# One fused block (modulated local attention and MLP) on one core: the hand-off order of 713 tasks and their buffer slots is replaced by another

## The chip, the core and the metric

The kernel runs on one core of a Trainium2 chip. The core's engines run side by side and meet only through semaphores: TensorE (PE) multiplies matrices and writes only to PSUM, VectorE (DVE), ScalarE (ACT) and GpSimd (POOL) do the rest of the arithmetic, and SyncE (SP) issues DMAs. Each engine takes its own instructions strictly in the order in which the program gives them. The metric is device time in microseconds; lower is better. Verdicts here call two kernels the same within 2%.

## What is computed

The input x has 2048 rows of 448 bfloat16 values. A vector c gives six modulation vectors. A layernorm, scaled and shifted by them, feeds an attention with 16 heads of 28 values in which row s looks at rows s, s−2, ..., s−14; its result is projected by wo, gated and added to x. A second modulated layernorm, and a third without modulation, feed an MLP of 1792 hidden values with a tanh GELU, gated and added again.

```python
mod = (_silu(c) @ w_mod).reshape(c.shape[0], 6, 1, -1)
sa, ca, ga, sb, cb, gb = (mod[:, i] for i in range(6))
h = _layernorm(x) * (1 + ca) + sa
qkv = (h @ wqkv)                       # 16 heads of 28; W, dil = 8, 2
idx = pos[:, None] - (jnp.arange(8) * 2)[None, :]
attn = softmax(where(idx >= 0, q . k[idx] * 28 ** -0.5, -1e9))
x = x + ga * ((attn . v[idx]) @ wo)
h = _layernorm(x) * (1 + cb) + sb
x = x + gb * (gelu(_layernorm(h) @ w1 + b1) @ w2 + b2)
```

## The kernel before

**Tiles.** The rows are split into even and odd ones, so that the dilated window becomes a plain window of 8 in each half. A tile p (0 to 7) is 128 even and 128 odd rows. `hT`, `qT` and `kT` hold the normalised rows, the queries and the keys with the features on the partitions.

**Stages.** For each tile DVE computes the statistics (L456 and L458) and normalises (L478); the reciprocal root of the variance is one power on POOL (L469) or two steps on ACT (L466, L467). A short copy, the "tail" (L488 to L492, on DVE, POOL or ACT), doubles the last 64 features. Tiles 0 and 1 are then transposed by PE (L535), tiles 2 to 7 by a DMA of SP (`zT`, L527), and scaled and shifted into `hT` (L502 on DVE, L504 on ACT; four per group of tiles, one for each quarter of the features). Queries and keys are projected by PE in two parts, full quarters (L548) and the remainder of 64 features (L554). For tiles 0 and 1 the result is copied straight into `qT` and `kT` (L609 on ACT, L610 on DVE). For tiles 2 to 7 it is copied into one of five staging buffers `zy` (L628 on ACT, L629 on DVE) and transposed into `qT` or `kT` by a DMA (L631).

The attention runs in nine batches of 114 positions of each half: values (L706 for batches 0 to 4; from a copied window `hw`, L689, and with L548 and L554 for 5 to 8), copied to `vb` (L721 on ACT, L724 on DVE); two sets of logits (`lt`, L738); exponentials (L745, ACT); mask (L751, DVE); denominators (`pd`, L760) and weighted values (`po`, L771); logarithm and exponential of the denominator (L780, L782, ACT); product (L788, DVE). The output projection (`pw`, L803) of a tile, the sum with x (L810) and the two layernorms (L819 applies the modulation) follow, and a transpose by DMA (`yT`, L834).

The MLP takes two tiles at a time, t = 0 to 3: 14 hidden tiles in pairs (g, g+7), two pairs to a group, named here by g: 0/1, 2/3, 4/5, 6. Each pair has full matmuls (L548) and remainder matmuls (L554) into one PSUM slot, and two GELUs on ACT (L864) that read that slot; the bias column for them is copied out of PSUM by DVE (L671). Then follow the second matmul (L883), the biased residual on POOL (L841, behind a gate L868) and the last add (L889) and the store (L893). Three phases interleave these: attention batches 0 to 4 and MLP 0, batches 5 and 6 and MLP 1, batches 7 and 8 and MLPs 2 and 3. ACT loads another table between exponentials and GELUs (L925, L932).

**What sets the order.** The code records 713 tasks (`Plan.add`), each with its engine, its inputs and outputs, and for some of them other engines that could do it (`alt`). Nothing is scheduled while the program is built. `emit` goes through a fixed list of task numbers, `ORDER`, and calls each; `:A`, `:D` and `:P` after a number put it on ACT, DVE or POOL, and `:R` reverses the two parts of a values task. So the list fixes each engine's order. `SLOTS` gives each buffer its slot among a few of its kind (`ROOM`): four PSUM slots P0 to P3 of two banks each (projections, logits, values, GELU inputs, all of them), five `zy`, two `et`, two `den`, two `hw` and so on. The first writer of a slot waits for all readers of the buffer that was in it before.

Of the kernel before, what the change touches and what calls it, by code (L numbers as in the profile page):

```python
# [14 lines left out]
S, D, H, DH, F = 2048, 448, 16, 28, 1792  # L15
# [25 lines left out]
ENGINE = {"A": "ACT", "D": "DVE", "P": "POOL", "R": "PE2"}  # L41
RATE = 310e3
SLOTS = [
# [6 lines left out]
]  # L50
ORDER = """
3 14 17 0 1 15 5 9 10 18 11 16 13 19 20 2 6 24 21 73 55+12@55 26 12 71 25 56 72 74 57 75 22 58 77 23 59 60 27 62 61 76
32 4 67 66 68+11@68 78 63 28 108 64 30 110 69 79 84:A 89:P 31 65 70 109 111 80 88:P 83 34 81 112:P 87:A 29 101+9@101
85 90:A 93:P 36 114 94+3@94 82 95 113 102 92:A 91 115:D 86 103 116 96 120:A 144 97 99 104 106 117:A 135 98 118:A 142
105 119:A 145 143 133 100 146 121 136 134 126 148 137 107 147 7 127 149:D 122 138 124 150 129 139 190 123 191 140 198
141 128 125 200 199 269 130 271 236 40 270 207 33 209 38 241 201 35 237 208 210 185 211 154 39 153 242 202 152 212
151:A 8 203 187 213 238 204 159 239 214:D 205 215 186 240 155 278 206 188 279 280 156 160 307:R 161 281 243 37 282 272
192 273:A 162 157 189 171 308:D 194 172 283 193 244 218 173 195 163 219 158 275 284 196 216 285 167 217 286 447:P 246
197 164 168 165 228 174 169:D 274 309 312 276:D 277 220 313 310 314 166 221 229 225 230 311 224 222:D 247 170 315 245
176 317 316 175 226 248 233 232 318 227 290 249 289:A 319 43 287:A 223 288 320 234 250 558:P 46 45 559 321 47 231 253  # L60
345 342 346 251 560 303 482:P 44 252 324 343 322 291 561 254 323 325 347 326 344 292 304 255 293 327 348 328 373:R 256
305 294 329 257 350 258 375 52 378 376 330 340:R 53 333 379 235 377 374 296 334 331 300 41 295 351 332 259 49 335 380
299 341 336 337 297 260 382 262 301 381 349 263 261 264 338:A 383 483 352 339 384 265 484 266 449 353 267 485 385 268
# [3 lines left out]
402 452 404 443 487 453 370 490 454 444 436 455 371:D 372 456 434 491 405 488 457 493 445 459 458 492 460 435 494 461  # L67
# [3 lines left out]
513 547 515:D 599 516 564 602 568 481 569 570 604 603 571 546 605 572 548 606 573 628 607 608 574 549 635 575 550 609  # L71
612 636 577 630 637 578 610 629 640 576 579 638 581 639 611 613 580 582 641 631 583 633 586 651 614 632 587 584 585
616 588 642 615 648 617 654 646 647 618 634 652 645 656 621 649 619 644 622 620 623 643 658 650 625 624 589 626 664
590 655 627 591:A 653 657 439 592 659 556 665 662 663 674 666 660 661 669 667 675 668 678 676 679 677 686 672 673 671
687 681 670 680 690 691 694 697 693 682 688 692 685 695 683 689 701 684 698 696 709 699 710 702 711 712 705 700 703
706 704 707 708
"""


# [883 lines left out]
```

## Time and profile before

| | us |
|---|---|
| median of 3 runs | 171.04 |
| the runs | 169.43, 171.04, 171.4 |
| span of the profiled execution, first to last instruction | 166.6 |
| what lies around the span, if that execution took the median | 4.4 |

The page gives the span of one execution but not its device time, so the last row is a difference between two executions. DVE and ACT are busy 116.1 and 102.4 us, POOL 46.7 us. DMA engines are nearly full for the first 62 us (all inputs and weights are loaded there, among the transposes) and near idle from then on. A row of the timeline has the start, the duration, the engine, the line, what is written from what, the count, and in brackets the idle time of that engine just before and what ended it. A row such as "1.78 ... x2" covers both instructions; the second starts about half of that after the first, so that rows of several give the rate at which an engine gets through them. PE's matmuls overlap, so their rate is read from where the next row starts.

### The profile page before, as it was taken

The page shows a single profiled execution, that of the slowest core. Times are in us where ns is not written, and L with a number is a line of the kernel's source. Part 1 is how long each engine was busy: PE and PEld are TensorE (multiplying, and loading weights), DVE is VectorE, ACT ScalarE, POOL GpSimd, SP SyncE. Part 2 cuts the span into 40 slices and gives each one's busy share as a digit, 9 for nine tenths or more (in the row PEclk, how much of TensorE's full clock was granted, in tenths as well). Part 3 has the DMA queues.
Part 4 walks back from the last instruction along what each step waited for, and adds up shares of the span by engine and source line. Part 5 has one row for each costly group of instructions (what it writes and reads, how often), then busy time and mean ns, then how long its engine had stood idle before and what let it go on. Part 6 is the DMA issues. An engine that isn't in the chain of part 4 may idle for free.

```text
span 166.6 us, 4971 instructions
## 1 busy us (share of the span) xinstructions
PE 160.9 (97%) x2126; PEld 83.7 (50%) x2126; DVE 116.1 (70%) x271; ACT 102.4 (61%) x142; POOL 46.7 (28%) x73
## 2 busy tenths in 40 slices
PE   6999899999999999999999999999999999999992
PEld 4678544444545543445555344556434455344572
DVE  6889899958899989996938886574788930500032
ACT  3378898798489953859674468947536820097300
POOL 3136332300261201289100114700002870007200
PEclk9999999999999999999999999999999999999999
DMA  5999989799999999900091000009010026110003
GB/s 152 323 335 311 182 269 172 147 160 190 222 185 306 147 161 245 151 0 6 2 139 46 4 0 0 4 0 126 8 55 0 0 55 185 64 46 0 0 1 110
DMA packets 35573, 18.78 MB, mean 113 GB/s; under 512 B 28507, under 2 KB 34592, under 8 KB 35552
## 3 DMA queue, kind: packets, MB, share of 16 engines
q1 hardware_dynamic: 35548, 18.47, 51.0%
q8 instruction: 16, 0.26, 0.7%
q14 instruction: 5, 0.04, 0.1%
q10 hardware_dynamic: 4, 0.00, 0.0%
HBM read 9.81 MB, written 1.84 MB: 70 GB/s over the span
## 4 chain that ended last, share of the span: by engine, by line
PE 88%; DMA 4%; ACT 2%; SPq 2%; POOL 1%; DVE 1%; issue 1%
PE p L883 26%; PE p L548 22%; PE pq L548 8%; PE pw L803 8%; PE pv L706 5%; PE p L554 4%; PE lt L738 4%; PE po L771 3%; PE pv L548 3%; DMA wqk_st<-in_A_wqkv_dram 3%; PE pq L554 2%; DMA kT<-zy 2%; PE pd L760 1%; SPq L349 1%; PE pb L641 1%
## 5 line engine op out<-in xcount | busy, mean ns | idle before, releaser
L864 ACT ACTIVATE hm<-p,b_col 128x512 bf16<-128x512 f32 x56 | 33.9, 692 | 29.9 <-PE p L554 27.3
L883 PE MATMUL p<-w_s,hm 128*128 128x448 bf16 (+1 forms) x238 | 44.1, 342 | 0.0
L548 PE MATMUL p<-yT,w_s 128*128 128x512 bf16 x168 | 38.1, 380 | 0.0
L469 POOL TENSOR_TENSOR rs_all<-mvs,neg_half 128x2 f32<-128x2 f32 x22 | 16.7, 764 | 58.0 <-DVE mvs L458 57.9
L883 PEld LDWEIGHTS <-hm 128*128 128x128 bf16 x238 | 22.6, 98 | 19.3 <-issue 0.8
L889 DVE TENSOR_TENSOR x_all<-p,x1p 128x896 bf16<-128x896 f32 (+2 forms) x10 | 8.9, 902 | 25.9 <-PE p L883 25.9
L548 PEld LDWEIGHTS <-w_s 128*128 128x128 bf16 x168 | 15.8, 98 | 20.9 <-issue 2.9
L456 DVE BATCH_NORM_STATS2 stt<-x_all 128x6 f32<-128x448 bf16 x32 | 18.6, 608 | 0.8 <-DMA x_all<-in_A_x_dram 0.6
L745 ACT ACTIVATE et<-lt 128x928 bf16<-128x928 f32 x18 | 16.0, 947 | 4.2 <-PE lt L738 3.9
L841 POOL TENSOR_TENSOR x1p<-x_all,gbb_bc 128x448 f32<-128x448 bf16 x16 | 17.8, 1137 | 0.0
L548 PE MATMUL pq<-wqk_st,hT 128*128 128x448 bf16 x72 | 15.0, 354 | 0.0
L788 DVE TENSOR_TENSOR qT<-po,den 128x912 bf16<-128x912 f32 x9 | 10.0, 1106 | 6.6 <-ACT den L782 6.4
L751 DVE TENSOR_TENSOR et<-et,mask 128x928 bf16<-128x928 bf16 x18 | 11.8, 683 | 3.1 <-ACT et L745 3.0
L803 PE MATMUL pw<-wo_s,qT 128*128 128x448 bf16 x64 | 13.3, 353 | 0.0
L780 ACT ACTIVATE den<-pd 128x928 f32<-128x928 f32 x9 | 8.5, 943 | 5.9 <-PE pd L760 5.7
L819 DVE TENSOR_TENSOR h<-h,mod_bc 128x896 bf16<-128x896 bf16 x16 | 11.1, 710 | 0.3
L628 ACT CAST zy<-pq 128x896 bf16<-128x896 f32 x10 | 8.9, 912 | 1.7 <-PE pq L554 0.9
L548 PEld LDWEIGHTS <-hT 128*128 128x128 bf16 x72 | 6.4, 98 | 6.9 <-issue 1.6
L782 ACT ACTIVATE den<-den,den_bias 128x928 f32<-128x928 f32 x9 | 9.6, 1072 | 0.2
L478 DVE TENSOR_SCALAR zy<-h,mvs,rs_all 128x448 bf16<-128x448 bf16 x16 | 6.6, 457 | 4.4 <-POOL rs_all L469 4.4
L810 DVE TENSOR_TENSOR x_all<-pw,x_all 128x896 bf16<-128x896 f32 x8 | 8.7, 1086 | 1.3 <-PE pw L803 1.3
L456 DVE BATCH_NORM_STATS2 stt<-h 128x6 f32<-128x448 bf16 x16 | 9.4, 612 | 0.2
(115 smaller groups left out, 182.0 us busy)
## 6 DMA issues: line engine op xcount, KB each, us to landing
w_s<-in_B_w_dram SPq DMA_DIRECT2D x7, 224.0 KB, 3.8
out_dram<-x_all SPq DMA_DIRECT2D x7, 224.0 KB, 2.1
x_all<-in_A_x_dram SPq DMA_DIRECT2D x3, 448.0 KB, 5.3
wmod<-in_w_mod_dram SPq DMA_DIRECT2D x3, 448.0 KB, 7.2
w_s<-in_B_w_dram SPq DMA_DIRECT2D x3, 448.0 KB
wqk_st<-in_A_wqkv_dram SPq DMA_DIRECT2D x3, 225.0 KB, 3.9
wm_st<-in_w_mod_dram SPq DMA_DIRECT2D x1, 672.0 KB, 4.6
x_all<-in_A_x_dram SPq DMA_DIRECT2D x2, 224.0 KB, 2.6
```

Of the source, the lines that this page charges most:

```text
L456: add("DVE", 0.53, lambda: nc.vector.bn_stats(out=stt[:, w, b, 0:6], in_=src()), reads=reads, bufs=bufs, after=early if w == b == 0 else ( ...
L469: ways = {"POOL": (0.55 + 0.17 * n, lambda: nc.gpsimd.tensor_tensor(out=r, in0=v, in1=neg_half[:, 0:n], op=ALU.pow))}
L548: nc.tensor.matmul(out(), lhsT=lhs(kt, slice(0, 128)), rhs=rhs(kt, slice(0, 128)), start=first and kt == 0, stop=not first and kt == KT - 2)
L554: nc.tensor.matmul(out(), lhsT=lhs(KT - 1, rows), rhs=rhs(KT - 1, rows), start=first, stop=not first, tile_position=(rows.start, 0))
L745: exps.append(add("ACT", 0.83, lambda half=half, lt=lt: nc.scalar.activation(out=et.t[:, 2 * half:2 * half + 2].rearrange("p r m c -> p r ...
L751: nc.vector.tensor_tensor(out=ev, in0=ev, in1=mask[:], op=ALU.mult)
L788: nc.vector.tensor_tensor(out=qT[:, :, LEAD + q00:LEAD + q00 + 2 * WQ], in0=po.t[:, :, 0:NS * 4 * WQ].rearrange("p j (m c) -> p m j c", c=WQ),
L803: nc.tensor.matmul(pw.t[:, s, 0:D], lhsT=qT[:, KT * s + ft, LEAD + 128 * p:LEAD + 128 * p + 128], rhs=wo_s[:, ft, :], start=(ft == 0), sto ...
L819: add("DVE", 0.55, lambda vec=vec, op=op: nc.vector.tensor_tensor(out=h2.t[:], in0=h2.t[:], in1=vec.unsqueeze(1).to_broadcast([128, NS, D] ...
L841: add("POOL", 1.0, lambda n=n: nc.gpsimd.tensor_tensor(out=x1p.t[:, n, :], in0=xn(p, n), in1=gbb2_bc[:], op=ALU.add), reads=[f"x{p}", "gbb ...
L864: gelus.append(add("ACT", 0.585, lambda f=f, a=a, p1=p1s[g]: nc.scalar.activation(out=hm.t[:, f].rearrange("p n c -> p (n c)"), in_=p1.t[: ...
L883: nc.tensor.matmul(p2.t[:, n, 0:c1 - c0], lhsT=hm.t[:, f, n, q * 128:(q + 1) * 128], rhs=w2_s[:, f, c0:c1], start=(f == parts[0][0]), stop ...
```

## The change

`SLOTS` and `ORDER` are replaced; all code, all tasks and the loads' sizes stay. [...] The first hundred or so tasks stand as before.

```diff
 SLOTS = [
-    0, 0, 1, 1, 0, 0, 0, 0, 1, 2, 3, 0, 1, 0, 2, 3, 0, 3, 2, 1, 0, 1, 0, 2, 3, 1, 2, 1, 2, 3, 4, 1, 1, 0, 0, 3, 0,
+    0, 0, 1, 1, 0, 0, 0, 0, 1, 2, 3, 0, 1, 0, 2, 3, 0, 2, 3, 3, 0, 1, 0, 3, 3, 1, 2, 1, 1, 0, 2, 2, 1, 2, 0, 1,
...
 ORDER = """
 3 14 17 0 1 15 5 9 10 18 11 16 13 19 20 2 6 24 21 73 55+12@55 26 12 71 25 56 72 74 57 75 22 58 77 23 59 60 27 62 61 76
 32 4 67 66 68+11@68 78 63 28 108 64 30 110 69 79 84:A 89:P 31 65 70 109 111 80 88:P 83 34 81 112:P 87:A 29 101+9@101
-85 90:A 93:P 36 114 94+3@94 82 95 113 102 92:A 91 115:D 86 103 116 96 120:A 144 97 99 104 106 117:A 135 98 118:A 142
+85 90:A 93:P 36 114 94+3@94 82 95 113 102 92:A 91 115:D 86 103 116 96 120:A 144 97 99 104 106 117:A 135 7 105 119:A
...
```

What that does to the engines shows in the order of the instructions. Three places matter below.

First, DVE at the start of the attention, from the statistics of tiles 2 and 3 to the scaling of these tiles into `hT` (L502). Before:

```order
L456 BN_STATS stt<-x_all 128x6
L458 BN_AGGR mvs<-stt 128x2 x2
L478 TENSOR_SCALAR zy_96<-x_all,mvs,rs_all 128x448 x2
L491 COPY zy_96<-zy_96 128x2x64
L478 TENSOR_SCALAR zy_97<-x_all,mvs,rs_all 128x448 x2
L456 BN_STATS stt<-x_all 128x6 x2
L458 BN_AGGR mvs<-stt 128x2
L456 BN_STATS stt<-x_all 128x6 x2
L458 BN_AGGR mvs<-stt 128x2
L456 BN_STATS stt<-x_all 128x6 x2
L458 BN_AGGR mvs<-stt 128x2 x3
L502 TENSOR_SCALAR hT<-zT,mod_col 128x2x256 x3
```

Now, in the same stretch:

```order
L456 BN_STATS stt<-x_all 128x6 x2
L458 BN_AGGR mvs<-stt 128x2 x2
L456 BN_STATS stt<-x_all 128x6
L478 TENSOR_SCALAR zy_96<-x_all,mvs,rs_all 128x448 x2
L456 BN_STATS stt<-x_all 128x6
L478 TENSOR_SCALAR zy_97<-x_all,mvs,rs_all 128x448 x2
L456 BN_STATS stt<-x_all 128x6 x3
L458 BN_AGGR mvs<-stt 128x2 x2
L456 BN_STATS stt<-x_all 128x6 x2
L478 TENSOR_SCALAR zy_96<-x_all,mvs,rs_all 128x448
L458 BN_AGGR mvs<-stt 128x2
L610 CAST kT<-pq 128x8x128
```

More statistics stand ahead of and between the normalisations of tiles 2 and 3, and behind all of it, ahead of L502, stands the copy of tile 1's keys, which ACT made before (L609). One of the three scalings of L502 goes to ACT.

Second, ACT in the middle of the attention, around the scaling of tiles 6 and 7 into `hT` (L504). Before:

```order
L780 ACTIVATE den<-pd 128x928
L628 CAST zy_97<-pq 128x32x28
L782 ACTIVATE den<-den,den_bias 128x928
L504 ACTIVATE hT<-zT,mod_col 128x2x256 x2
L628 CAST zy_100<-pq 128x32x28
L745 ACTIVATE et<-lt 128x928 x2
```

Now:

```order
L628 CAST zy_96<-pq 128x32x28
L628 CAST zy_100<-pq 128x32x28
L780 ACTIVATE den<-pd 128x928
L782 ACTIVATE den<-den,den_bias 128x928
L504 ACTIVATE hT<-zT,mod_col 128x2x256 x3
L628 CAST zy_98<-pq 128x32x28
L504 ACTIVATE hT<-zT,mod_col 128x2x256
L628 CAST zy_96<-pq 128x32x28
L745 ACTIVATE et<-lt 128x928 x2
```

All four scalings of these tiles are on ACT now. The copy of tile 4's queries (to `zy_98`) moved from ahead of the reciprocal to behind three of them, and the copy of tile 5's queries (to `zy_96`) behind the fourth.

Third, PE in the first group of the MLP. The number behind `p1` is the buffer. Before, the full matmuls of group 4/5 (`p1_1649` takes the slot of a pair of group 2/3, whose GELUs it waits for) come behind the twelve full matmuls of group 0/1 (`p1_1616` is its second pair), whose remainders were done ahead of them:

```order
L548 MATMUL p1_1616<-yT_1534,w1_s_76 128x512
L548 LDWEIGHTS w1_s_76
L548 MATMUL p1_1616<-yT_1534,w1_s_76 128x512
L548 LDWEIGHTS w1_s_76
L548 MATMUL p1_1649<-yT_1534,w1_s_76 128x512 [waits Activation_49]
```

Now the remainders of group 0/1 (`p1_1621` is its second pair, in P3) come last and those of group 4/5 right behind (`p1_1650` in P1, `p1_1653` in P3):

```order
L554 MATMUL p1_1621<-yT_1470,w1_r_77 128x512
L554 LDWEIGHTS w1_r_77
L554 MATMUL p1_1650<-yT_1470,w1_r_77 128x512
L554 LDWEIGHTS w1_r_77
L554 MATMUL p1_1650<-yT_1470,w1_r_77 128x512
L554 LDWEIGHTS w1_r_77
L554 MATMUL p1_1653<-yT_1470,w1_r_77 128x512 [waits Activation_49]
```

The wait for ACT, for the two GELUs that read the slot P3, now stands three matmuls behind the last matmul that these GELUs need. In the third MLP ACT's GELUs also stand in another order: one of the first pair of group 0/1 stands between the two of its second pair.

More of the change, by code (lines that the diff above doesn't have):

```diff
@@ L53 @@
 32 4 67 66 68+11@68 78 63 28 108 64 30 110 69 79 84:A 89:P 31 65 70 109 111 80 88:P 83 34 81 112:P 87:A 29 101+9@101
-85 90:A 93:P 36 114 94+3@94 82 95 113 102 92:A 91 115:D 86 103 116 96 120:A 144 97 99 104 106 117:A 135 98 118:A 142
-105 119:A 145 143 133 100 146 121 136 134 126 148 137 107 147 7 127 149:D 122 138 124 150 129 139 190 123 191 140 198
-141 128 125 200 199 269 130 271 236 40 270 207 33 209 38 241 201 35 237 208 210 185 211 154 39 153 242 202 152 212
-151:A 8 203 187 213 238 204 159 239 214:D 205 215 186 240 155 278 206 188 279 280 156 160 307:R 161 281 243 37 282 272
@@ L58 @@
[L58 to L62, printed above, removed]
@@ L63 @@
-299 341 336 337 297 260 382 262 301 381 349 263 261 264 338:A 383 483 352 339 384 265 484 266 449 353 267 485 385 268
[3 rows of a table removed]
-402 452 404 443 487 453 370 490 454 444 436 455 371:D 372 456 434 491 405 488 457 493 445 459 458 492 460 435 494 461
[3 rows of a table removed]
-513 547 515:D 599 516 564 602 568 481 569 570 604 603 571 546 605 572 548 606 573 628 607 608 574 549 635 575 550 609
-612 636 577 630 637 578 610 629 640 576 579 638 581 639 611 613 580 582 641 631 583 633 586 651 614 632 587 584 585
-616 588 642 615 648 617 654 646 647 618 634 652 645 656 621 649 619 644 622 620 623 643 658 650 625 624 589 626 664
@@ L74 @@
-590 655 627 591:A 653 657 439 592 659 556 665 662 663 674 666 660 661 669 667 675 668 678 676 679 677 686 672 673 671
-687 681 670 680 690 691 694 697 693 682 688 692 685 695 683 689 701 684 698 696 709 699 710 702 711 712 705 700 703
-706 704 707 708
+85 90:A 93:P 36 114 94+3@94 82 95 113 102 92:A 91 115:D 86 103 116 96 120:A 144 97 99 104 106 117:A 135 7 105 119:A
+142 98 118:A 136 145 133 107 127 122 269 121 134 100 143 280 123 146 137:A 187 147 190 148 200 126 149:A 191 150 139
+128 138 271 188 140 124 129 8 278 236:R 141 125 198 201 199 207 202:A 33 185 237 209 35 203 37 270 130:D 38 151:A 154
@@ new lines @@
+241 153 152:A 238 208 272 210 242 204 159 211 205:A 273 213 186 206 155 279 212 281 189 214:A 239 192 215 160 156
+161:D 171 157 193 243 172 158 307 240 282:A 195 284 162 244 196 308:D 194 167 39 246 219 217 173 283 218:A 163 197 40
+285:A 216:A 286 247 275 168 221 164 169:D 229 165 174 228 274 276:D 277 309 312 310 220 166 313 311 232 222 314 170
+176 230 245 315 223 233 248 225 317 224 175 318 41 316 288:A 249 319 290:A 289:A 226 320 250 287:A 227 234 558:P 251
+345 321 342 231 482:P 303 343 322 346 46 253 292 560 44 252 304 254 291 347 305 47 255 323 43 324 559 42 257 293 325
@@ new lines @@
+256 235 326 258 375 259 378 260 45 340:R 379 262 376 327 344 373 561 328 329 341 330 296 263 348 333 374 295 377 350
+331 299 332 334 297 380 335 447 349 351 337 381 261 300 336 484 383 264 352 483 338 384 339 266 265 382 267:D 406
+593:P 353 385 268 485:D 386 51 52 354 53 448 49 301:D 48 50 355 131 449 414 54 132 387 413 294 357 356 390 298 358 183
+359 388 407 416 450:D 177 415 302 418 178 417 391 361 360 426 389 408 181 420 392 182 412 425 411 394 180 410 393 419
[3 rows of a table added]
+467 464 465 500 596:D 468 469 470 518 526 502 503 528 504 529 471 527 505 472 519 506 531 520 475 530 521 473 540 544
@@ new lines @@
+522 523 543 553 542 534 533 507 535 551 508 532 474 510 557 511 509 476 512 565 597 562 541 598 554 477 513 563 514
+545 566 564 515:A 567 552 516 478 479 599 600 568 555 601 547 570 480:D 602 481 571 569 604 603 572 548 605 606 573
+628 607 546 608 549 574 635 575 609 610 636 612 630 576 640 611 613 577 629 614 639 578 579 637 580 615 581 616 617
+641 634 618 632 619 633 582 638 583 631 621 648 642 620 622 586 647 645 623 584 646 651 625 658 585 587 649 624 588
+643 653 644 656 650 652 626:A 627 662 589 590 591 654 592 663 655 556 664 659 665 657 674 660 666 661 667 675 550 669
@@ L77 @@
+679 668 676 678 677 680 671 670 672 690 692 673 687 694 681 686 684 691 683 685 697 693 688 689 695 682 709 698 696
+710 699 701 711 700 712 702 439 705 703 706 704 707 708
 """
```

19 rows, old and new, of tables (ORDER, SLOTS) are left out of this document.

## The prediction, made before the changed kernel was run

> **What bounds the kernel now.** I read the page first, then the busy time by stage, then who waits for whom on PE, and then the timeline around each place that the change touches.
>
> ```profile
> span 166.6 us, 4971 instructions
> PE 160.9 (97%) x2126; PEld 83.7 (50%) x2126; DVE 116.1 (70%) x271; ACT 102.4 (61%) x142; POOL 46.7 (28%) x73
> ...
> PE 88%; DMA 4%; ACT 2%; SPq 2%; POOL 1%; DVE 1%; issue 1%
> ```
> ```profile
> 0.00:11.00 11.00, 9.21 (x89) 6.72 (x90) 9.01 (x50) 4.91 (x11) 3.54 (x15) 1.00 0.85 258
> 11.00:43.30 32.30, 31.35 (x617) 17.45 (x616) 27.82 (x64) 26.67 (x34) 8.69 (x16) 1.00 0.96 208
> 43.30:62.80 19.50, 19.49 (x378) 9.97 (x378) 18.34 (x41) 15.42 (x19) 4.75 (x6) 1.00 1.05 209
> 62.80:121.00 58.20, 58.20 (x813) 28.80 (x812) 44.05 (x85) 38.17 (x50) 17.34 (x21) 1.00 0.31 51
> 121.00:166.60 45.60, 42.65 (x236) 20.79 (x234) 16.89 (x35) 17.24 (x29) 12.39 (x15) 0.99 0.16 47
> ```
> ```profile
> PE pv L706 <- ACT qT L609: 0.5, 1, 0.5
> PE po L771 <- issue: 0.3, 1, 0.3
> ```
>
> The reader is to see that PE is the whole story. The columns of the second fence are the stretch, then the busy time of PE, weight loads, DVE, ACT and POOL, and the granted clock. From 11.0 to 43.3 us PE is idle 0.95 us, from 43.3 to 121.0 us 0.01 us. Of the last 2.95 us nearly all lies after the last matmul. In the third fence 0.55 and 0.34 us are the only waits of PE after 11 us that are worth a name (a further 0.5 us, for a transposed k, counts as a weight load's: below). So a new order of the same instructions can take away about 1.4 us (0.8%) after 11 us, and every wait that it adds on PE is paid in full. The first 11 us stand in the same order in both kernels and stay.
>
> The sum is made against the span of this execution, 166.6 us. That is 4.4 us under the median of the runs, 171.04 us. I take the difference as launch and end and carry it over.
>
> **The change part by part.** No computation is added or removed, and PE's instructions are the same ones. 29 small tasks change engine: five scalings go from DVE to ACT, seven copies from PSUM and eleven tails change between engines, and four powers and two window copies. I walked the new order engine by engine, each instruction starting when its engine, its inputs and its PSUM slot were free, with the durations of the trace. Six places change PE's idle time.
>
> *1. Start of the attention.* These rows give the durations:
>
> ```profile
> 11.71 1.68 DVE L456 BATCH_NORM_STATS2 stt<-x_all 128x6 f32<-128x448 bf16 x3 [0.59 <-DMA x_all<-in_A_x_dram]
> 12.40 2.79 PE L548 MATMUL pq<-hT,Wqk 128*128 128x256 bf16 x24
> 13.76 1.47 POOL L469 TENSOR_TENSOR rs_all<-mvs,neg_half 128x2 f32<-128x2 f32 x2 [3.60 <-DVE mvs L458]
> 14.44 1.04 ACT L609 CAST kT<-pq 128x1024 bf16<-128x1024 f32 x1
> 15.34 0.70 DVE L478 TENSOR_SCALAR zy<-x_all,mvs,rs_all 128x448 bf16<-128x448 bf16 x2
> 15.49 2.72 SPq L527 DMA_TRANSPOSE zT<-zy  x2
> 18.07 1.64 PE L706 MATMUL pv<-Wv,hT 128*64 128x448 bf16 x16 [0.55 <-ACT qT L609]
> 20.01 1.64 PE L706 MATMUL pv<-Wv,hT 128*64 128x448 bf16 x16
> 20.34 1.70 DVE L502 TENSOR_SCALAR hT<-zT,mod_col 128x512 bf16<-128x512 bf16 x3 [0.78 <-DMA zT<-zy]
> 21.58 0.70 PE L738 MATMUL lt<-qT,kT 28*64 28x58 bf16 x64
> 22.27 2.44 PE L548 MATMUL pq<-wqk_st,hT 128*128 128x448 bf16 x12
> 31.71 1.09 DVE L629 CAST zy<-pq 128x896 bf16<-128x896 f32 x1
> ```
>
> The wait of 0.55 us goes, since v of batch 1 now follows further projections and finds its slot free. Next late is the key of tile 1. Its copy from PSUM moves from ACT (1.04 us) to DVE, where it would take about 1.2 us (1.09 us × 1024/896). On DVE there now stand ahead of it, counted from 13.30 us (three statistics from 11.71 at 0.53 us each), nine statistics of 0.53, seven aggregates of about 0.1, five normalisations of 0.31, and about 0.7 us of waiting (0.4 for POOL's power of 0.73 us, 0.3 for a transpose to free its buffer): 4.8 + 0.7 + 1.55 + 0.7 = 7.7. The copy runs from 21.0 to 22.2 us. PE is through with all that lies ahead of the logits of batch 1 at 17.5 (18.07 − 0.55) + 0.37 (one more set of logits) + 3.14 (two v) = 21.0 us, and waits 1.2 us. The logits end at 22.9. The next projections need the transposed tiles 2 and 3. The second transpose is issued at 18.2 instead of 16.9 us, because DVE now normalises in another order, lands about 3.4 us later as before (16.9 to 20.3), at 21.6, and then two scalings follow on ACT, to 23.1. The first matmul goes ahead of the second scaling. PE is at the place of 22.27 us at about 23.1: **+0.8 us** (0.5 to 1.2 by the landing).
>
> *2. Logits of batch 2.* Here before waits 0.50 us for a transposed key; now the transposes are in time, but slot P1 comes free only after ACT's copy of k of tile 3 behind a reciprocal, at about 34.7 against 34.2 us on PE. A wait of 0.5 gives way to one of 0.5: **0**.
>
> ```profile
> 32.97 0.59 PEld L738 LDWEIGHTS <-kT 28*64 28x64 bf16 x64 [0.50 <-DMA kT<-zy]
> ```
>
> *3. Projections of tiles 6 and 7.* ACT now has four scalings ahead of them where it had two, and two copies between.
>
> ```profile
> 28.56 0.94 ACT L780 ACTIVATE den<-pd 128x928 f32<-128x928 f32 x1
> 29.53 1.07 ACT L782 ACTIVATE den<-den,den_bias 128x928 f32<-128x928 f32 x1
> 40.12 3.33 PE L803 MATMUL pw<-wo_s,qT 128*128 128x448 bf16 x16
> 43.28 1.30 PE L548 MATMUL pv<-Wv,hw 128*128 128x448 bf16 x6
> 40.46 1.51 ACT L504 ACTIVATE hT<-zT,mod_col 128x512 bf16<-128x512 bf16 x2
> 48.22 1.71 ACT L628 CAST zy<-pq 128x896 bf16<-128x896 f32 x2 [0.63 <-PE pq L554]
> 78.35 3.45 ACT L745 ACTIVATE et<-lt 128x928 bf16<-128x928 f32 x4
> ```
>
> PE was through with its two output projections at 43.28 before, so now at about 44.15. Two sets of logits (0.35 each) take it to 44.85. ACT, from the logits of batch 2 at 35.1: two exponentials (0.84), two copies (0.81), logarithm and exponential of the denominator (0.97 each, the first when PE has made it, at 38.8), then three scalings (0.71), a copy, the fourth scaling and a copy: 38.8 + 1.94 + 2.13 + 0.81 + 0.71 + 0.81 = 45.2. That last copy frees P1 for the projection: PE waits about **+0.45 us** (0 to 0.9, since the buffer of that copy also waits for a transposed key).
>
> *4. Logits of batch 4.* They need slots P2 and P1, freed by ACT copies that first wait until the transposes of q of tile 4 and k of tile 5 have left their buffers. On SP those two are issued only at 44.1 and 45.5 us, since q of tile 4 is now copied behind the scalings of place 3, and k of tile 5, copied long before, stands behind it in SP's queue (before, they went at about 39.5 and at 45.3). What a transpose takes:
>
> ```profile
> DMA to landing us min/median/max: 4.7/5.0/5.8
> ```
> ```profile
> 29.64 0.05 issue
> 29.70 3.23 DMA kT<-zy
> 32.93 0.04 issue
> ```
>
> With 3.23 us k of tile 5 lands at 48.7, its buffer is filled again by 49.6, and PE, at 49.8, doesn't wait. With 5.8 us it lands at 51.3 and PE waits 2.2 us. The queue ahead holds only transposes and a small row, which speaks for the short end; the large weight loads come right behind. I take **+0.6 us** (0 to 2.2).
>
> *5. First GELU matmuls.* The bias column's copy on DVE now stands behind a copy of 1.09 us and a statistic, and one of the first two PSUM slots waits for it: **+0.25 us** (0 to 0.5).
>
> *6. Reuse of PSUM among the GELU matmuls.* In the first MLP the remainder matmuls of hidden tiles 4/5 follow right behind those of tiles 0/1 and write into the slot P3 that tile 1's GELUs are still to read. They can't start earlier, since the remainder completes the sum.
>
> ```profile
> 65.49 1.04 PE L554 MATMUL p<-yT,w_r 64*128 64x512 bf16 x8
> 66.35 2.42 ACT L864 ACTIVATE hm<-p,b_col 128x512 bf16<-128x512 f32 x4 [2.87 <-PE p L554]
> 62.80 2.75 PE L548 MATMUL p<-yT,w_s 128*128 128x512 bf16 x12
> ```
>
> Four GELUs take 2.42 us, so 0.58 each and 0.1 for the way. Two of them take 1.35 us with both ways; two remainder matmuls (0.24 us, of 8 in 0.96) go into P1 beside them. PE waits **+1.1 us** (0.5 if a half slot is enough, which the trace of before doesn't show; nowhere there does PE wait at this point). In the third MLP the full matmuls of tile 5 need P1, which holds tile 1: ACT runs tile 1's second GELU, one of tile 0 and then tile 1's first, 1.9 us after the last matmul with the ways, and the matmuls of tile 4 cover 1.33 (six at 0.22): **+0.55 us** (0 to 0.8).
>
> Everything else I cost at nothing. The moved POOL rows (window copies, biased residuals) lie 3 us or more ahead of their readers; if that cover goes, a 1.04 us row is paid. The stores and the loads of the second weights moved on SP: w2 is scaled on DVE by 76 us, PE wants it at 77. The last fourteen matmuls, the last add and the last two stores stand as before.
>
> Sum: 0.8 + 0 + 0.45 + 0.6 + 0.25 + 1.1 + 0.55 = 3.75 us. Span 170.35, time 171.04 + 3.75 = **174.8 us**, 2.2% slower.
>
> [...] Row first: the granted clock is 1.00 in the stretch that holds the waits of 0.55, 0.50 and 0.34 us. [...]
>
> **The rivals.** *Fast transposes, not slower by 2%.* All transposes land in 3.2 us. Then place 4 costs nothing and place 1 0.2 less, and the time is 171.04 + 2.95 = 174.0 us. It decides when k of tile 5 lands less than 3.7 us after its issue. For it: the row of 3.23 us. Against it: the row's median of 5.0.
>
> *Late transposes.* They take 5.8 us, place 4 costs 2.2, place 3 0.9: 171.04 + 5.8 = 176.8 us. For it: that row's largest value, with weight loads beside it.
>
> [...]
>
> *No difference, or faster.* The execution profiled may be one with few late transfers; an order that is less exposed to them would gain in the other runs (they spread from 169.4 to 171.4 us), and the waits of before go: 171.04 − 1.4 and up to 1.6 more, 168.0 to 169.6 us. Against it: place 6 hangs on no transfer and costs more than the 1.4.
>
> **How the numbers follow.** A measurement of this kernel can tell about 2%, that is 167.6 and 174.5 us. Forecast as walked (174.5 to 175.8): 0.34. Late transposes: 0.16. Clock: 0.05. Fast transposes, with a term or two at its lower bound (171.0 to 174.4): 0.37. No difference or faster: 0.08, of which 0.03 below 167.6. Slower by over 2%: 0.34 + 0.16 + 0.05 = 0.55; within 2%: 0.37 + 0.05 = 0.42; faster: 0.03. Range: down to 171.5 us, which leaves out the last rival and the end of the fast one, and up to 178.0. The forecast's own range is 174.5 to 175.8.
>
> **What would show it.** In the new profile: step 1, an idle spell on PE of about 1.2 us before logits (L738) at 21 us, ended by DVE's copy (L610), and L548 on hT starting near 23.1; step 3, 0.45 us at 45 us, ended by ACT L628; step 4, a wait near 50 us whose length tells the landing; step 6, 1.1 us within L554 near 72 us and about 0.5 us within L548 near 131 us, both ended by ACT L864. The prediction is wrong if PE's idle time from 11 to 121 us is under 3 us, if the clock's digits fall, or if PE waits where I have no term, at the output projections (L803) above all, or for the transposed yT of a later MLP, which has 0.3 us to spare at 96 us.

## The result: 177.96 us, and the profile after

| | before | after |
|---|---|---|
| median | 170.71 | 177.96 |
| the runs | 169.43, 170.39, 171.04, 171.4 | 174.93, 177.15, 178.77, 179.46 |
| span of the profiled execution | 166.6 | 175.3 |

The changed kernel is slower: the ratio is 1.034 (95% interval 1.024 to 1.044). The ratio leaves out two of the four executions of the changed kernel, those more than 1.5% above its fastest, and the medians don't. The device time of the profiled execution is 177.15 us, so only 1.85 us lie around its span.

First the page of the changed kernel, then its busy time by stage (the columns are those of the table before: PE, weight loads, DVE, ACT, POOL, granted clock):

```profile
span 175.3 us, 4977 instructions
PE 162.3 (93%) x2126; PEld 84.0 (48%) x2126; DVE 117.0 (67%) x269; ACT 103.4 (59%) x150; POOL 42.8 (24%) x69
...
PE 62%; DMA 16%; ACT 8%; DVE 8%; issue 3%; POOL 1%; SPq 0%; ACTq 0%; DVEq 0%; POOLq 0%
```
```profile
0.00:11.00 11.00, 8.07 (x75) 5.82 (x76) 7.99 (x46) 3.84 (x9) 3.23 (x15) 0.84 0.80 244
```

The chain that ended last was 88% PE. Now transposes and loads (DMA), the work of ACT and DVE, and "issue" hold a third of it. In the first 11 us, where PE's order is the same in both kernels, the clock is 0.84. What PE waited for:

```profile
PE lt L738 <- DVE kT L610: 2.6, 1, 2.6
PE ps_col L410 <- DMA wm_r<-in_w_mod_dram: 1.5, 1, 1.5
...
PE p L554 <- ACT hm L864: 1.1, 1, 1.1
PE pd L760 <- issue: 1.0, 1, 1.0
PE lt L738 <- ACT zy L628: 0.7, 1, 0.7
PE p L548 <- ACT hm L864: 0.6, 1, 0.6
PE pq L548 <- ACT zy L628: 0.4, 1, 0.4
PE pw L803 <- DVE qT L788: 0.2, 1, 0.2
PE pq L554 <- DVE qT L788: 0.2, 1, 0.2
PE p L554 <- DVE b_col L671: 0.2, 1, 0.2
```

L610 is place 1, L628 places 4 (0.7) and 3 (0.4), L671 place 5, L864 place 6. Four rows have no term in the forecast: `wm_r`, 1.0 us of "issue", that is, PE waits for nothing the profile shows, and two of 0.2 us for L788, one of them at an output projection (L803). The timeline at place 1:

```profile
18.30 2.87 SPq L527 DMA_TRANSPOSE zT<-zy  x2
19.39 3.15 PE L706 MATMUL pv<-Wv,hT 64*64 64x448 bf16 x32
23.50 0.40 DVE L478 TENSOR_SCALAR zy<-x_all,mvs,rs_all 128x448 bf16<-128x448 bf16 x1 [1.49 <-DMA zT<-zy]
23.91 1.18 DVE L610 CAST kT<-pq 128x1024 bf16<-128x1024 f32 x1
25.15 0.70 PE L738 MATMUL lt<-qT,kT 28*64 28x58 bf16 x64 [2.61 <-DVE kT L610]
25.79 2.44 PE L548 MATMUL pq<-wqk_st,hT 128*128 128x448 bf16 x12
```

DVE stands 1.49 us in front of a normalisation, until a transpose issued at 18.30 has left its buffer (5.1 us later). Behind that normalisation stands the key copy (L610), and PE waits for the copy.

### The profile page after: what moved, and what is told of

The parts are those of the page before. It is cut to its first block, busy times and chain, and to the rows that moved or that the text cites. A ratio compares the mean times of both kernels' runs of the same rounds, so it can differ in the third digit from the quotient of the medians.

```text
span 175.3 us, 4977 instructions
## 1 busy us (share of the span) xinstructions
PE 162.3 (93%) x2126; PEld 84.0 (48%) x2126; DVE 117.0 (67%) x269; ACT 103.4 (59%) x150; POOL 42.8 (24%) x69
## 4 chain that ended last, share of the span: by engine, by line
PE 62%; DMA 16%; ACT 8%; DVE 8%; issue 3%; POOL 1%; SPq 0%; ACTq 0%; DVEq 0%; POOLq 0%
PE p L883 25%; PE p L548 20%; DMA zT<-zy 6%; PE p L554 4%; DMA qT<-zy 4%; PE pq L548 4%; PE pw L803 3%; DMA x_all<-in_A_x_dram 3%; DMA wm_st<-in_w_mod_dram 3%; ACT hm L864 3%; ACT zy L628 2%; PE lt L738 2%; PE po L771 2%; DVE stt L456 2%; ACT hT L504 2%
## 5 line engine op out<-in xcount | busy, mean ns | idle before, releaser
L864 ACT ACTIVATE hm<-p,b_col 128x512 bf16<-128x512 f32 x56 | 34.1, 690 | 39.0 <-PE p L554 27.6
L548 PE MATMUL p<-yT,w_s 128*128 128x512 bf16 x168 | 38.6, 379 | 0.7 <-ACT hm L864 0.6
L469 POOL TENSOR_TENSOR rs_all<-mvs,neg_half 128x2 f32<-128x2 f32 x20 | 15.3, 769 | 64.4 <-DVE mvs L458 64.3
L548 PEld LDWEIGHTS <-w_s 128*128 128x128 bf16 x168 | 15.8, 98 | 21.9 <-issue 4.5
L751 DVE TENSOR_TENSOR et<-et,mask 128x928 bf16<-128x928 bf16 x18 | 11.2, 633 | 9.0 <-ACT et L745 9.0
L841 POOL TENSOR_TENSOR x1p<-x_all,gbb_bc 128x448 f32<-128x448 bf16 x16 | 16.6, 1067 | 0.2 <-POOL seen L868 0.2
L548 PE MATMUL pq<-wqk_st,hT 128*128 128x448 bf16 x72 | 15.0, 353 | 0.4 <-ACT zy L628 0.4
L788 DVE TENSOR_TENSOR qT<-po,den 128x912 bf16<-128x912 f32 x9 | 9.9, 1104 | 5.3 <-ACT den L782 3.5
L803 PE MATMUL pw<-wo_s,qT 128*128 128x448 bf16 x64 | 13.3, 353 | 0.2 <-DVE qT L788 0.2
L819 DVE TENSOR_TENSOR h<-h,mod_bc 128x896 bf16<-128x896 bf16 x16 | 10.2, 651 | 0.2
L478 DVE TENSOR_SCALAR zy<-h,mvs,rs_all 128x448 bf16<-128x448 bf16 x16 | 8.0, 520 | 2.9 <-POOL rs_all L469 2.9
L548 PEld LDWEIGHTS <-hT 128*128 128x128 bf16 x72 | 6.5, 98 | 7.0 <-issue 1.7
L738 PE MATMUL lt<-qT,kT 28*64 28x58 bf16 x576 | 6.4, 192 | 3.3 <-DVE kT L610 2.6
```

The lines of the kernel that those rows point to most:

```text
L469: ways = {"POOL": (0.55 + 0.17 * n, lambda: nc.gpsimd.tensor_tensor(out=r, in0=v, in1=neg_half[:, 0:n], op=ALU.pow))}
L548: nc.tensor.matmul(out(), lhsT=lhs(kt, slice(0, 128)), rhs=rhs(kt, slice(0, 128)), start=first and kt == 0, stop=not first and kt == KT - 2)
L738: nc.tensor.matmul(lt.t[WK * j:WK * j + WK, r % 2, c0:c0 + WE], lhsT=kT[HP * r:HP * r + DH, m, k0:k0 + WK], rhs=qT[HP * r:HP * r + DH, m, ...
L751: nc.vector.tensor_tensor(out=ev, in0=ev, in1=mask[:], op=ALU.mult)
L788: nc.vector.tensor_tensor(out=qT[:, :, LEAD + q00:LEAD + q00 + 2 * WQ], in0=po.t[:, :, 0:NS * 4 * WQ].rearrange("p j (m c) -> p m j c", c=WQ),
L803: nc.tensor.matmul(pw.t[:, s, 0:D], lhsT=qT[:, KT * s + ft, LEAD + 128 * p:LEAD + 128 * p + 128], rhs=wo_s[:, ft, :], start=(ft == 0), sto ...
```

## The experiments

Each edits the order list; times are medians. "Clock" is the mean granted clock of a whole execution; a stretch of 3.4 us at half clock brings it from 1.00 to 0.99.

### The same kernels again

No edit. First the changed kernel:

> The changed kernel once more, unedited. Theory (waits set by the order): the waits on PE for the key copy L610 (2.6 us), for the copies L628 (0.7 and 0.4) and for the GELUs L864 (1.1 and 0.6) stand again within 0.3 us of these values, and the time is 1.03 to 1.04 of the kernel before. The 1.5 us wait for wm_r in the first 11 us, where both kernels have the same order, belongs to one execution and is under 0.5 us here. Rival (late transfers of one execution): the waits for copies that follow a transpose change by over 0.5 us and the time is within 2% of before.

Measured: 178.03 us, against 170.25 for the kernel before on the same chip (11 runs, 168.5 to 170.43). The six took 174.93 us at clock 1.00, and 177.96 to 178.64 at 0.99 in the other five. The profile is that of the first. Its PE waits:

```profile
PE lt L738 <- DVE kT L610: 2.5, 1, 2.5
...
PE p L554 <- ACT hm L864: 1.1, 1, 1.1
PE lt L738 <- ACT zy L628: 0.7, 1, 0.7
PE p L548 <- ACT hm L864: 0.6, 1, 0.6
PE pq L548 <- ACT zy L628: 0.4, 1, 0.4
PE pd L760 <- issue: 0.4, 1, 0.4
```

The waits that the order makes stand within 0.1 us of the first profile; that for `wm_r` is gone, as expected. But this is the profile of the execution that took 3 us less than the other five. The time expected, 1.03 to 1.04, was exceeded: 178.03/170.25 is 1.046. Something that differs by execution was still missing, and the clock pointed to it. The next two are one more execution of each kernel:

> The changed kernel, unedited, in another execution. Five of six timed ones had a span of 176.1 to 176.7 us and a mean granted clock of 0.99, one (the profiled) 173.1 and 1.00. Theory (the wait of 2.5 us for L610 makes the clock fall in most executions): a stretch of about 3.4 us at half clock begins between 22 and 28 us, costs about 1.7 us, and the rest of the 3.1 us is a later start of the full clock in the first 11 us. Rival (late transfers): the clock is full from 11 us on and the 3.1 us lie in waits for DMA.

> The kernel before, unedited, in another execution. In 11 timed executions beside the first four runs its span was 166.8 to 168.7 us, ten of them 167.8 or more, where the profile that the forecast was made from had 166.6. Theory (that profile was one with a short head): the first projection of batch 0 (L548 on Wqk) starts 1 to 1.5 us later than 12.40, because PE's clock is granted in full later, and the spacing behind it is the same within 0.5 us. Rival (transfers are late in the middle): the head is the same and the time lies at waits for transposes or for instructions at 30 to 45 us.

The changed kernel: 178.31 us, span 176.5, clock 0.98. Windows of 3.41 us of its profile, and two rows of the timeline:

```profile
4.37:7.78 3.41, 1.83 (x20) 1.26 (x19) 2.07 (x13) 0.88 (x4) 0.00 (x0) 1.00 1.05 335
7.78:11.20 3.42, 3.42 (x45) 2.83 (x43) 3.02 (x14) 1.94 (x5) 2.04 (x4) 0.50 0.94 295
...
21.44:24.85 3.41, 1.89 (x79) 1.06 (x75) 2.32 (x7) 2.20 (x4) 0.00 (x0) 1.00 0.83 256
24.85:28.26 3.41, 3.41 (x15) 1.48 (x11) 2.38 (x10) 2.99 (x6) 1.39 (x2) 0.50 0.72 178
28.26:31.67 3.41, 3.41 (x44) 1.21 (x42) 2.36 (x4) 2.08 (x5) 0.00 (x0) 1.00 0.49 95
```
```profile
24.18 0.70 PE L738 MATMUL lt<-qT,kT 28*64 28x58 bf16 x64 [1.52 <-DVE kT L610]
24.82 4.12 PE L548 MATMUL pq<-wqk_st,hT 128*128 128x448 bf16 x12
```

The number behind POOL is the clock: full, then 0.50 for one row of 3.41 us, twice. The first fall follows the wait for `wm_r` (1.48 us here), the second the wait for the key copy (1.52 us). The twelve projections behind it take 4.12 us instead of 2.44. So the theory's place and price, 1.7 us, are seen in this execution. A wait of 1.67 us for "issue" comes on top.

The kernel before: 170.49 us, span 168.8. Here the theory was wrong and the rival right: the head, the time up to the first projection of batch 0, is not longer (12.28 us against 12.40). The 2.2 us against the profile of the forecast lie in the middle, in waits for copies and scalings:

```profile
PE po L771 <- ACT zy L628: 0.7, 1, 0.7
...
PE pq L548 <- DVE hT L502: 0.5, 1, 0.5
PE lt L738 <- DVE zy L629: 0.4, 1, 0.4
PE pq L548 <- ACT hT L504: 0.4, 1, 0.4
```

One more execution of the changed kernel:

> The changed kernel, unedited, in one more execution, to see how often which fall of the clock comes. Theory: a stretch of half clock that begins at 21 to 28 us, behind the wait for L610; span 176 to 177 us. Rival (the falls lie in the first 11 us, behind the late wm_r): no half clock after 12 us.

175.3 us, span 173.4, clock 1.00: no fall at all, so neither side was seen. The key copy was waited for 1.6 us and "issue" 1.8. Over all twelve executions of the changed kernel, nine had a clock of 0.99 or less (177.15 to 179.46 us) and three 1.00 (174.93, 174.93, 175.3). Of the 32 executions of the kernel before that were timed beside these experiments, one had 0.99. But where a fall lies is known for two of the nine only: in the profile of 177.15 us it lies in the head alone (7.34 to 10.76 us, behind `wm_r`), in that of 178.31 us in the head and at place 1. So place 1 as the cause rests on the experiments that follow.

### Work in the wait: is the clock the cause?

```diff
 ORDER
...
-236:R 185 241 238 159
+236:R 185 241+16@159 238 159
...
```

(PE's entries alone.) `241+16@159` puts 16 matmuls on constants into the slot of task 159 ahead of the logits, task 241.

> The changed kernel with 16 matmuls on constants (L382, 0.11 us each, 1.8 us in all) on PE ahead of the logits of batch 1, where PE waits 2.5 us for the key copy L610. They write a PSUM slot that is free and that the projection behind writes anew. Theory (that wait makes the clock fall): the clock stays at 1.00 in all executions and the median falls from 178.0 to 176.3 us (175.0 to 176.8), although PE has more to do. Rival (the clock has no part, late transfers have): the clock is 0.99 in most executions as before and the median stays within 0.6 us of 178.0.

Measured: 174.99 us (174.47 to 175.47), ratio to before 1.030 (1.025 to 1.034), clock 1.00 in all six. PE does 1.9 us more work and the median is 3.0 us under the unedited 178.03, just below the range expected. The 178.03 comes from another chip, on which the kernel before takes 0.5 us longer; each against its own kernel before, the gain is 2.5 us. And 174.99 is level with the unedited executions at full clock (174.93 to 175.3): what the work takes away are the falls.

```profile
20.88 1.92 PE L382 MATMUL pq<-warm_w 128*128 128x256 bf16 x16
23.04 0.70 PE L738 MATMUL lt<-qT,kT 28*64 28x58 bf16 x64 [0.25 <-DVE kT L610]
23.68 2.44 PE L548 MATMUL pq<-wqk_st,hT 128*128 128x448 bf16 x12
```

The projections run at full speed. The theory holds for the clock; the gain is 0.8 to 1.3 us larger than the 1.7 of one half-clock stretch. The profile also has no "issue" wait here, where the unedited kernel's profiles show 0.4 to 1.8 us; whether that is the rest was not separated.

### The converse: the same wait in the kernel before

```diff
 ORDER
...
-141 128 125 200 199 269 130 271 236 40 270 207 33 209 38 241 201 35 237 208 210 185 211 154 39 153 242 202 152 212
+141 128 125 200 199 269 271 236 40 270 207 33 209 38 201 35 237 208 210 211 154 130:D 241 185 39 153 242 202 152 212
...
```

The copy of tile 1's keys (130) goes from ACT to DVE and behind a scaling; 241 and 185 only keep their place behind it, PE's order is unchanged.

> The converse: the kernel before, with the copy of tile 1's keys on DVE (L610) behind the first scaling of L502 instead of on ACT (L609), so that PE waits about 2.5 us for it ahead of the logits of batch 1, as in the changed kernel; nothing else moves. Theory (one such wait costs its length and, in most executions, a stretch of half clock): 170.25 + 2.5 + up to 1.7 = 172.7 to 174.5 us, 1.015 to 1.025, with a mean clock of 0.99 in most executions. Rival (the slack behind it absorbs the wait): under 171.5 us. Rival (the clock has no part): 172.7 us and 1.00.

Measured: 171.92 us (171.5 to 173.35) against 169.75, ratio 1.014 (1.009 to 1.018), clock 0.99 in five of six. That is under the range expected, though not in the slack. In its profile the wait was only 1.1 us, since PE itself came 2.4 us later out of the head, and the fall of the clock lay there, from 9.45 to 12.87 us, behind two waits of 0.5 and 0.4 us that the edit didn't make. One more execution:

> The kernel before with the late key copy of tile 1, in one more execution: in five of six timed ones the clock was 0.99, and in the profiled one the fall lay in the first 13 us, behind a late wm_r, with a wait of 1.1 us for L610. Theory (where the head is short, the wait is 2 to 2.5 us and the clock falls there): head as in the kernel before, a wait of about 2.5 us, half clock from 21 to 28 us. Rival (the late copy never makes the clock fall): no half clock after 13 us.

172.74 us, and the theory's fall:

```profile
22.55 0.44 PE L738 MATMUL lt<-qT,kT 28*64 28x58 bf16 x32 [2.06 <-DVE kT L610]
```
```profile
20.56:23.98 3.42, 1.43 (x44) 0.93 (x44) 3.03 (x8) 1.81 (x3) 1.78 (x3) 1.00 0.93 304
23.98:27.39 3.41, 3.41 (x77) 1.74 (x74) 0.88 (x4) 2.15 (x4) 0.29 (x1) 0.50 0.51 108
```

One copy put late takes the clock down in the kernel before as well, in this one profile; the five at 0.99 above don't show it, since the only one of them with a profile fell in the head.

### The GELU slots alone

```diff
 ORDER
...
-408 181 420 392 182 412 425 411
+408 181 392 182 412 425 420 411
...
-634 618 632 619 633 582
+634 618 633 619 632 582
...
```

> The changed kernel with two edits in the MLPs: the remainder matmuls of group 4/5 of the first MLP stand behind the full matmuls of group 6 again, and in the third MLP both GELUs of tile 1 stand ahead of that of tile 0. Theory: PE's waits of 1.1 us (L554) and 0.6 us (L548) for L864 go, nothing takes their place, and the time falls by 1.7 us, 1.0% of before. Rival (ACT's GELUs are the bound there, so PE waits for the next ones instead): the two waits go, others of the same size come up within the same MLP, and the time falls by under 0.5 us.

Measured: 175.29 us (174.54 to 176.92), clock 0.99 in two of six. Both waits are gone and no other came up in their MLPs. From its first matmul to its first second-layer matmul MLP 0 now takes 11.65 us (68.27 to 79.92) against 12.74 in the profile of the unedited kernel at full clock, MLP 2 11.22 against 11.80: 1.7 us, as the theory says. The median fell by more, 2.7 us, with fewer falls of the clock (five of six before), though the edits lie far behind place 1. The profiled span shows none of it, 173.2 against 173.1: the head was 1.2 us longer, and this row has another 1.7 (2.10 against 0.38):

```profile
41.97 0.38 PE L760 MATMUL pd<-et,ones_k 64*32 64x464 bf16 x6 [2.10 <-issue]
```

### Mending DVE's order, and all places together

```diff
 ORDER
...
-134 100 143 280 123
+134 100 143 123
...
-237 209 35 203 37 270 130:D 38
+237 209 130:D 35 203 37 38
...
-279 212 281 189
+212 269 271 270 272 273 280 278 279 281 189
...
```

(269, 271, 272, 273 and 278 go out of their old places on other lines: these are the statistics of tile 6 with their aggregates and their power.)

> The changed kernel with DVE's start of the attention mended: the copy of tile 1's keys (L610) stands ahead of the first normalisation of tile 4, which waited for a transpose, and the four statistics of tile 6 stand behind the normalisations of tiles 4 and 5. Theory: the 2.6 us wait of the logits goes down to under 0.3 us; the projections behind them then wait for the transposed tiles 2 and 3, which are issued about 0.6 us earlier; the time falls by 1.4 us (0.8 to 2.0), 0.8% of before. Rival (the transposes land late whatever DVE does): the wait only moves to L548 with its whole length, and the time falls by under 0.4 us.

Measured: 176.51 us (175.53 to 178.95), clock 0.99 in two of six. The median fell by 1.5 us, as the theory says, but the profile at full clock is no shorter (173.6 us against 173.1), so this isn't the theory's gain; there are fewer falls here. The wait for L610 is gone and the projections of tile 2 start at 22.99 us, 1.5 earlier than in the full-clock profile of the unedited kernel, although PE waited 1.4 us for a late `Wv`. But at the values behind them, at 28.55 us against 28.57, the start was given back:

```profile
27.42 1.08 DVE L629 CAST zy<-pq 128x896 bf16<-128x896 f32 x1
28.55 1.64 PE L706 MATMUL pv<-Wv,hT 128*64 128x448 bf16 x16 [0.61 <-DVE zy L629]
```

DVE has the moved statistics to do ahead of here (23.73 to 26.2 us), and the copy that frees the slot for the next values starts at 27.42 us, as it did unedited (27.43). Neither theory nor rival: the earlier start was real and was lost 6 us later on the same engine.

With these edits, those of the GELUs, the copy of tile 4's queries ahead of the scalings and two scalings on DVE:

> The edits of the two runs before together, and in the middle of the attention the copy of tile 4's queries ahead of the scalings of tiles 6 and 7, two of the four scalings on DVE again. Theory: 1.7 + 1.4 + about 0.8 (waits of 0.4 and 0.7 us for L628, some of it taken back by DVE's two scalings) = 3.9 us less than the changed kernel, that is 1.010 to 1.015 of before. Rival (the loss is spread over transfers, not over these places): less than 2 us, 1.022 or more.

Measured: 175.43 us (174.35 to 177.13), ratio 1.031 (1.026 to 1.036). Far from the 1.010 to 1.015 of the theory; the median is 2.6 us lower than unedited, between theory and rival, and the clock is 0.99 in three of six. PE's rows tell why: place 1 moved on to the transposed tiles, and place 3 grew.

```profile
PE pq L548 <- ACT hT L504: 1.8, 2, 1.5
...
PE pq L548 <- ACT zy L628: 1.1, 1, 1.1
```
```profile
45.64 0.91 ACT L628 CAST zy<-pq 128x896 bf16<-128x896 f32 x1 [2.04 <-PE pw L803]
```

ACT stood 2.04 us ahead of the copy that was moved up. The row names the output projection as what came last, but the copy doesn't read it: its input was done at 43.2 us, and its buffer `zy` held tile 3's queries, whose transpose was issued at 40.72. So I read it as the copy moved forward into a transpose that had not landed; no run tested that alone.

### What adds up

```diff
 ORDER
...
-237 209 35 203 37 270 130:D 38
+237 209 130:D 35 203 37 270 38
...
```

This and the GELU edits, without work in the wait:

> The changed kernel with the copy of tile 1's keys ahead of the first normalisation of tile 4 (nothing else moved on DVE, no matmuls on constants) and both edits of the GELU slots. Theory (a wait stays at place 1, now for the transposed tiles, since these were issued late; it is 1 to 1.6 us and so makes the clock fall in fewer executions): L610 isn't waited for any more, L548 waits 1.0 to 1.6 us for L504, the clock is 0.99 in up to half of the executions, 174.5 us (173.3 to 175.5). Rival (the key copy alone was place 1): no wait above 0.5 us at 20 to 26 us, clock 1.00, 172.5 us or less.

Measured: 175.02 us (174.01 to 176.4), clock 0.99 in five of six, more than expected. L548 waits 1.2 + 0.3 us for L504, L610 0.5; the profile falls to half clock from 24.87 to 28.28 us. The time is within the range expected. With the key copy out of the way these waits were left, and in this profile a fall came behind them.

And the work in the wait of place 1 together with the GELU edits:

> The changed kernel with the 16 matmuls on constants in the wait of place 1 and with both edits of the GELU slots (place 6). Theory (the two causes are apart and add up): 175.0 - 1.7 = 173.3 us (172.7 to 173.9), clock 1.00 in all executions; waits for L864 on PE under 0.1 us. What is left over the kernel before, some 3 us, is then the late start of tile 2's projections, the waits of 0.4 and 0.7 us for L628 and the spread of transfers. Rival (the gain of the GELU edits in the first run was a gain in clock only): 174.5 us or more.

Measured: 173.81 us (172.9 to 175.21) against 169.68, ratio 1.024 (1.018 to 1.031), clock 1.00 in all. The median is within the theory's range at its upper side, and the profiled span is 171.5 against 173.2 without the GELU edits. This is the fastest version of the changed kernel here; none beats the kernel before (the interval of this one reaches under the 2% that counts as the same).

## Why the forecast was right on the direction and 3.2 us short

Where PE starts, in us, from the timelines (second column: the other execution of the kernel before; third and fourth: the changed kernel at full clock and with two falls):

| | before, forecast's profile | before | after, clock 1.00 | after, 0.98 | with work and GELU edits |
|---|---|---|---|---|---|
| L548 of batch 0 | 12.40 | 12.28 | 12.26 | 14.04 | 12.21 |
| L548 of tile 2 | 22.27 | 22.64 | 24.52 | 24.82 | 24.82 |
| MLP 0, first matmul | 62.80 | 64.95 | 66.55 | 69.91 | 66.64 |
| MLP 0, second layer | 73.80 | 75.95 | 79.29 | 82.67 | 78.29 |
| MLP 2, first matmul | 120.26 | 122.41 | 125.91 | 129.28 | 124.91 |
| MLP 2, second layer | 131.26 | 133.41 | 137.71 | 141.08 | 136.13 |
| span | 166.6 | 168.8 | 173.1 | 176.5 | 171.5 |

The direction came out, and the median lies in the stated range, 0.04 us under its end of 178.0. That is luck: the sum forecast 174.8 us, the range reached far enough for late transposes (176.8) and for a fall of the clock (176.5, at the price measured below), and falls, with a chance of 0.05, are what happened. By one of its own signs, "if the clock's digits fall", the prediction was wrong: the clock of the first 11 us fell to 0.84.

*The clock: the step that failed.* The sum has no term for the clock; what had been measured was a clock of 1.00 beside waits of 0.55 us and less, and that waits near 1 us leave it alone as well was the author's assumption. The chance of 0.05 stood for one or two stretches of half clock, and the profile of before shows none up to its last matmul, so neither their length nor their price. The runs showed 3.41 us each at a clock of 0.50, and at place 1 a price of 1.7 us (4.12 against 2.44 us for the same twelve projections); one or two of these on 174.8 make 176.5 or 178.2 us, and the median lies between. The wait at place 1 was 1.5 to 2.6, and nine of twelve executions had a fall. Both directions were shown: with work in the wait none of twelve executions fell (two experiments) and the median of the first of them was 2.5 to 3.0 us lower, and in the kernel before the late copy alone made the clock fall in one profile.

*Place 1, mis-sized.* The mechanism is as walked: the key copy on DVE behind blocked normalisations, then the transposed tiles. The term was +0.8 us; between the second and third columns it is 24.52 − 22.64 = 1.9 (against the forecast's profile 2.25, and 2.4 with the head, which is 0.14 shorter). The walk gave DVE 0.3 us for a transpose to free its buffer, and it stood there 1.49 and 1.50 us; it let the second transpose land 3.4 us after its issue, the waits show 4.4 to 5.1. That row came from an execution with quick transposes: those of L527 landed in 3.6 us (median) there, in 5.0 in the first profile of the changed kernel. Why they differ wasn't separated; loads run beside them.

*Places 2 to 5* were sized well as waits: 0, 0.45, 0.6 and 0.25 forecast; nothing seen at place 2, and 0.4, 0.7 and 0.2 at the others. At place 4 the mechanism holds too, as in the profile of 174.93 us, where ACT's two copies wait for a transposed q:

```profile
50.30 1.81 ACT L628 CAST zy<-pq 128x896 bf16<-128x896 f32 x2 [1.57 <-DMA qT<-zy]
```

But they are not losses against the other execution of before. From tile 2 to MLP 0 the changed kernel takes 42.03 us at full clock, the kernel before 40.53 in the forecast's profile and 42.31 in the other. "Every wait that it adds on PE is paid in full" fails here: against that execution these waits cost nothing, since it has waits of the same sort. That its span of 168.8 us is nearer to a usual one than 166.6 is seen from those of the 32 (166.7 to 171.0 us, half of them above 168.4); the waits of the 32 weren't seen.

*Place 6* holds: 1.1 and 0.55 us forecast, 1.14 and 0.64 seen, both taken out by the edit that names their cause. The stretches are 1.74 and 0.80 us longer than before, and with the edits still 0.65 and 0.22; this rest wasn't traced.

*The base.* "I take the difference as launch and end and carry it over": 4.4 us. In the other profiled execution of the kernel before it is 1.69 us. So the one that the forecast was made from took about 168.3 us, by that difference, and was one of the fastest, not a median one. Here errors cancelled: the base was 2.7 us too high, place 1 and the rest of MLP 0 and 2 too low, and the sum of 174.8 met the three executions without a fall (174.93 to 175.3) by luck.

*The sum at full clock.* From the second column to the third: 1.9 us more up to tile 2, 0.3 less from there to MLP 0, 1.7 more in it, 0.2 more up to MLP 2, 0.8 more in it, nothing behind. That is 4.3 us, the difference of the spans, where 3.75 was forecast. The 3 us on top come with the falls.

*Rivals.* Late transposes had 0.16 for 176.8 us; they came late at place 1, but places 3 and 4 stayed near their forecast sizes, so that rival's mechanism isn't what made 178. The gap between executions at 0.99 and at 1.00 is 3 us, of which one fall at place 1 is 1.7. In the one profiled near 178 us (fourth column) the stretch from tile 2 to MLP 0 is 3.1 us longer, by 1.7 for the fall and 1.3 for a longer "issue"; its fall in the head delays batch 0 by 1.8 us but tile 2 by 0.3 only, since the wait at place 1 is shorter. Whether "issue" is the rest in the other eight stays open; and one of the 32 executions of the kernel before took 172.69 us at clock 1.00, so some 3 us can come without a fall, too.

## What to carry to other kernels

In this kernel a wait of 1.5 to 2.6 us on TensorE cost its length, and where a fall of the clock came behind it another 1.7 us (nine of twelve executions had a fall, at this place or another); price it so, and try a filler of matmuls in a free slot when the wait can't be removed (174.99 us with it here, 178.03 without). Before a sum is made against a profile, see whether that execution is a usual one: its device time, not the median, belongs to its span. An instruction moved forward gained here only up to the next thing that was late: the projections of tile 2 started 1.5 us earlier, the values behind them at 28.55 us against 28.57. Look for that thing before such an edit is priced.

## What was not expected of the hardware

*Each fall to half clock lasted 3.41 us, and where it lay differed by execution.* The six seen run from 7.34 to 10.76, 7.78 to 11.20, 9.45 to 12.87, 24.85 to 28.26, 23.98 to 27.39 and 24.87 to 28.28 us; the two of one execution (7.78 and 24.85) start 17.07 us apart, five times 3.41. In the 3.41 us ahead of the last three PE was busy for 1.89, 1.43 and 1.55 us, a third to a half of it logits of 28 rows. In the full-clock profile of the changed kernel the clock stayed at 1.00. The wait of 2.48 us lies in two stretches of 3.41 us, if these are laid as here; no fall marks where they lie:

```profile
19.32:22.73 3.41, 1.99 (x20) 0.92 (x16) 1.91 (x8) 1.60 (x4) 0.00 (x0) 1.00 1.35 153
22.73:26.15 3.42, 2.26 (x73) 1.54 (x74) 2.84 (x11) 3.13 (x5) 1.35 (x2) 1.00 0.84 281
26.15:29.56 3.41, 3.41 (x45) 1.29 (x42) 3.41 (x8) 3.21 (x8) 0.04 (x1) 1.00 0.80 153
```

Busy time alone doesn't decide: the first profile of the changed kernel kept its clock behind a stretch of 1.55 us busy, all with values (L706), and the kernel before with the late key copy lost it behind one of 2.42 us:

```profile
20.99:24.41 3.42, 1.55 (x18) 0.72 (x15) 1.93 (x5) 1.42 (x4) 0.00 (x0) 1.00 1.15 142
```
```profile
6.04:9.45 3.41, 2.42 (x46) 1.80 (x45) 2.31 (x13) 0.92 (x2) 0.66 (x2) 1.00 0.97 271
9.45:12.87 3.42, 3.42 (x17) 2.38 (x17) 2.55 (x11) 2.13 (x5) 1.50 (x3) 0.50 0.95 307
```

Four of the six falls followed one wait of 1.5 to 2.1 us, one (24.87 us) waits of 0.5, 1.2 and 0.3, and one (9.45 us) two of 0.5 and 0.4. What decides whether the clock falls was not shown.

*PE waits for "issue" behind the same count of matmuls, in both kernels.* The rows run from the start to that wait, of the kernel before and of the changed one:

```profile
0.00:37.97 37.97, 35.24 (x607) 21.39 (x607) 32.30 (x107) 27.17 (x40) 11.19 (x30) 1.00 0.94 229
```
```profile
0.00:41.96 41.96, 35.26 (x607) 21.59 (x607) 31.30 (x103) 28.88 (x49) 7.99 (x25) 0.96 0.90 207
```

Both times 607 matmuls were done, with different matmuls around. The waits were 0.34 and 1.00 us. In other profiles they were 0.4 to 2.1 in six of the changed order and its edits and none in three (both with work in the wait, and that with all places mended), and none to 0.6 in the old order. What PE waits for there was not shown.
